# A decode block with attention and MLP: the last 64 columns of the output rows in shared products

## The chip, the cores and the metric

One NeuronCore of a Trainium2 chip runs the kernel. The metric is device time in microseconds (us), the median of several runs. The profile is one execution of the same program with the hardware profiler; its lines name an engine: PE is the matrix engine, PEld its weight loads, DVE the vector engine, ACT the scalar engine, POOL GpSimd, and SP the engine that only issues DMAs here. L483 is line 483 of the kernel before.

## What is computed

Two sequences (B = 2) with one new token each, D = 576. A gate g mixes an attention over a cache with an MLP:

```python
g = sigmoid((x * gate_w).sum(-1))
q = x @ wq                          # 32 heads of 128
p = softmax(q @ k_cache.T * 128**-0.5)   # 4096 cached keys a head
a = (p @ v_cache) @ wo              # 4096 -> 576
b = gelu(x @ w1 + b1) @ w2 + b2     # 576 -> 4608 -> 576
out = g * a + (1 - g) * b
```

Everything is float32. The two caches hold 134 MB each; with the weights 308.6 MB are read once.

## The kernel before

**The ring.** All large data pass through one SBUF tile, `ring`, of 49152 floats in each partition, in three slots of 16384 floats: 0 to 16383, 16384 to 32767, 32768 to 49151. First wq and w1 fill floats 0 to 39167. What lies behind them, from 39168 on, is handed out piece by piece by `temp()` (L159) to short-lived tiles of the first stage: x, the biases, transposes, the MLP's hidden row. They lie in the third slot.

**The order of the loads.** A list `seq` (L100 to L104) holds every load in order: wq, w1, then k and v of 16 units (a unit is four heads of one sequence, 8.4 MB of keys and as much of values), and three last loads with rows of w2 and wo. `load()` (L171) takes the next from the list and issues it on SP's queue. k of unit 0 (k0 below) goes to slot 0, v0 to slot 1, k1 to slot 2, v1 to slot 0 and so on. The first eight loads stand at fixed places in the program: five near the start, k0 at L298, v0 at L375 and k1 at L394. From then on `load_next` (L188) issues a load when the load three places before it, whose slot it takes, has been read for the last time.

**The order of the instructions** on each engine is the order of the program (a manual schedule). Accesses to parts of a tile that overlap are ordered by semaphores in the order of the program; parts that don't overlap are independent.

**The first stage** ends with the MLP's hidden values `hg` (L393), the load of k1 (L394), and a few small tiles (L396 to L407): `mod4`, `div4` and `hm` on DVE, a product of PE on the last two, and its copy `hx`. They split the last row group of w2 in four for the rows "wx". `mod4`, `div4` and `hm` have places of their own in pool `cp`. The gate sums L473 to L477 follow.

**The units** (L559 to L577): DVE multiplies the whole k slot by q in place (`mul`, L483), DVE and POOL sum over the head dimension (`red`, L487 to L489), a maximum goes over PE (L498) and DVE (L502), ACT exponentiates (L508), PE multiplies by v (`av`, L519, four groups of 32 output partitions in turn), and DVE and PE collect the result (L531, L537). In iteration i DVE does `mul` and `red` of unit i, PE `av` of unit i-1. v of unit i+1 takes the slot of k of unit i and is issued after `red(i)`; k of unit i+2 takes the slot of v of unit i and is issued after `av(i)`.

**The output rows.** w2 (36 rows of 576 columns in each partition, the last split as "wx") and wo (32 rows) come in the three last loads. Every row is multiplied by a weight of two columns, one for each sequence, and summed in PSUM tile `acc`. `acc_mm` (L351) splits the 576 columns in two products of 288; row r goes to partition groups 64 * (r % 2) and 32 behind it, so that four products in a row lie in four groups of 32 partitions. A float32 product is two instructions of PE in the profile. `mlp_out` and `wo_out` call it for w2 and wo; 24 of w2's rows stand ahead of `av` of the last unit, the others between the steps of the last normalization (L579 to L598).

**The end** (`last_out`, L435): `acc` is copied by ACT to `sums`; wo's rows from 23 on go to another tile `res` in four products of 144 columns each; after row 26 `fold` adds the four groups of `sums` to `res`; row 31 comes last, and copies and one DMA write the output. `late()` hands out places in the slot of the last load, behind its data.

Of the kernel before, what the change touches and what calls it, by code (L numbers as in the profile page):

```python
# [19 lines left out]
def kernel(  # L20
# [14 lines left out]
    nc = tc.nc  # L35
    B, H, SK, DH = k_cache.shape
    D = x.shape[-1]
# [21 lines left out]
    NC = 4  # L59
    DO = D // NC  # L60
    NS = 2
    DS = D // NS
    SCALE = float(DH) ** -0.5
    SLOTS = 3

    LAST = (
        (("w2", 0, 14), ("w2", 14, 28)),
        (("w2", 28, 35), ("wx", 0, 4), ("wo", 0, 9), ("wo", 9, 17)),
        (("wo", 17, 23), ("wo", 23, 27), ("wo", 27, 30), ("wo", 30, 31), ("wo", 31, 32)),
    )  # L70
    FOLD = 23
    SLOT = R * DH
# [8 lines left out]
    cp = ctx.enter_context(tc.tile_pool(name="cp", bufs=1))  # L81
# [4 lines left out]
    ps_acc = ctx.enter_context(tc.tile_pool(name="ps_acc", bufs=1, space=bass.MemoryType.PSUM))  # L86
    ps_av = ctx.enter_context(tc.tile_pool(name="ps_av", bufs=2, space=bass.MemoryType.PSUM))
    ps_big = ctx.enter_context(tc.tile_pool(name="ps_big", bufs=1, space=bass.MemoryType.PSUM))
    ps_o = ctx.enter_context(tc.tile_pool(name="ps_o", bufs=1, space=bass.MemoryType.PSUM))
# [6 lines left out]


    ring = rp.tile([P, SLOTS * SLOT], F32, name="ring")
    kt, vt, wqt, w1t, rows = {}, {}, {}, {}, {}
    seq = [(w, c) for w in ("wq", "w1") for c in range(len(ROWS[w]) + 1)]  # L100
    for i in range(N):
        seq += [("k", i), ("v", i)]
# [19 lines left out]
    def slot(n):  # L122
        k = len(held) % SLOTS
        return ring[:, k * SLOT:k * SLOT + n]
# [12 lines left out]
    def load_last(m):  # L137
        n = sum(z - a for _, a, z in LAST[m]) * D

        used["e"], used["z"] = len(held) % SLOTS * SLOT + n, (len(held) % SLOTS + 1) * SLOT  # L140
        t = slot(n)
        o = 0
        for w, a, z in LAST[m]:
            if w == "wx":
                x2 = t[:32, o:o + z * D]
                rows[w] = x2
                o += z * D
                for c in range(4):
                    nc.sync.dma_start(x2[c::4].rearrange("e (s n) -> e s n", s=4), srcx2[c])
                continue  # L150

            ends = (a * D, a * D + DS, a * D + DS + DO, z * D) if (w, z) == ("wo", 32) else (a * D, z * D)
            for u, v in zip(ends, ends[1:]):
                nc.sync.dma_start(t[:, o:o + v - u], srcs[w][:, u:v])
                o += v - u
            for r in range(a, z):
                rows[w, r] = t[:, o - (z - r) * D:o - (z - r - 1) * D]

    def temp(n, parts=P):  # L159
        t = ring[:parts, used["t"]:used["t"] + n]  # L160
        used["t"] += n
        assert used["t"] <= SLOTS * SLOT
        return t

    def late(n, parts=P):
        t = ring[:parts, used["e"]:used["e"] + n]
        used["e"] += n
        assert not seq and used["e"] <= used["z"]
# [28 lines left out]
    b2r = temp(D, 1)  # L197
# [17 lines left out]
    ident = cp.tile([P, P], F32, name="ident")  # L215
# [3 lines left out]
    idsc = cp.tile([P, P], F32, name="idsc")  # L219
    nc.vector.tensor_scalar_mul(idsc, ident, SCALE)  # L220

# [4 lines left out]
    NO = N * E  # L226
    pt = []
    for j in range(NPB):
        t = cp.tile([P, NT * EB + 32 - EB], F32, name=f"p{j}")
# [39 lines left out]
    g1 = cp.tile([P, B], F32, name="g1")  # L269
# [76 lines left out]

    acc = ps_acc.tile([P, DS], F32, name="acc")

    def acc_mm(lhsT, rhs, k, start=False, stop=False):  # L351
        m = lhsT.shape[-1]
        for s in range(NS):
            o = 64 * (k % 2) + 32 * s
            nc.tensor.matmul(  # L355
                acc[o:o + m], lhsT, rhs[:, s * DS:(s + 1) * DS], start=start, stop=stop, skip_group_check=True
            )

    g1z = cp.tile([1, 2, 32], F32, name="g1z")
    nc.vector.memset(g1z, 0.0)  # L360
    nc.vector.tensor_copy(g1z[:, 0, :B], g1[0:1])
    for k in range(2):
        acc_mm(g1z[:, k], b2r, k, start=True)

    fold = cp.tile([P, NS, B], F32, name="fold")
    nc.vector.tensor_add(
        fold, ident[:, :P // 2].rearrange("p (s c) -> p s c", s=NS)[:, :, :B],
        ident[:, P // 2:].rearrange("p (s c) -> p s c", s=NS)[:, :, :B],
    )


    hps = [ps_av.tile([P, 512], F32, tag="av", name=f"hps{m}") for m in range(FB - 1)]
# [12 lines left out]
    hg = cp.tile([P, NF, B], F32, name="hg")  # L385
    t = temp(NF * B).rearrange("p (r b) -> p r b", b=B)
# [6 lines left out]
    nc.vector.tensor_mul(hg, t, g1.unsqueeze(1).to_broadcast([P, NF, B]))  # L393
    load()  # L394

    mod4 = cp.tile([P, 4], F32, name="mod4")  # L396
    nc.vector.tensor_reduce(mod4, ident.rearrange("p (q s) -> p s q", s=4), AX.X, ALU.add)
    div4 = cp.tile([P, 32], F32, name="div4")
    nc.vector.tensor_reduce(div4, ident.rearrange("p (q s) -> p q s", s=4), AX.X, ALU.add)
    hm = cp.tile([P, 4, B], F32, name="hm")  # L400
    nc.vector.tensor_mul(
        hm, hg[:, NR:].to_broadcast([P, 4, B]), mod4.unsqueeze(2).to_broadcast([P, 4, B])
    )
# [2 lines left out]
    hx = cp.tile([32, 4, B], F32, name="hx")  # L406
    nc.vector.tensor_copy(hx.rearrange("p s b -> p (s b)"), hxps)  # L407

    def mlp_x():
        for s in range(4):  # L410
            acc_mm(hx[:, s], rows["wx"][:, s * D:(s + 1) * D], s)

    def mlp_out(lo, hi):
        for r in range(lo, hi):
            acc_mm(hg[:, r], rows["w2", r], r)

    KB = DH // 32
    oP = cp.tile([P, B, 32], F32, name="oP")  # L420

    def o_turn(turn):
        t = late(B * 32).rearrange("p (b c) -> p b c", c=32)
        for b in range(B):
            nc.vector.transpose(t[:, b], oT[:, b])
        ps = ps_sm.tile([P, B * 32], F32, tag="sm", name="op_t")
        nc.tensor.matmul(ps, turn, t.rearrange("p b c -> p (b c)"), start=True, stop=True)
        nc.vector.tensor_copy(oP.rearrange("p b c -> p (b c)"), ps)

    def wo_out(lo, hi):  # L430
        for r in range(lo, hi):
            acc_mm(oP[:, :, r], rows["wo", r], r)


    def last_out():  # L435
        res = ps_big.tile([32 * (NC - 1) + B, DO], F32, tag="big", name="res")
        sums = late(DS)
        nc.scalar.copy(sums, acc)

        def part(r, s):  # L440
            nc.tensor.matmul(  # L441
                res[32 * s:32 * s + B], oP[:, :, r], rows["wo", r][:, s * DO:(s + 1) * DO],
                start=r == FOLD, stop=r == 31, skip_group_check=True,
            )

        for r in range(FOLD, 31):
            for s in range(NC):
                part(r, s)
            if r == FOLD + 3:
                for s in range(NC):  # L450
                    h, o = divmod(s * DO, DS)
                    nc.tensor.matmul(
                        res[32 * s:32 * s + B], fold[:, h], sums[:, o:o + DO],
                        start=False, stop=False, skip_group_check=True,
                    )

        osb = late(D, B)
        for h in ((0, 1), (2,), (3,)):
            for s in h:
                part(31, s)  # L460
            for s in h:
                cpy = nc.vector.tensor_copy if s % 2 == 0 else nc.scalar.copy
                cpy(osb[:, s * DO:(s + 1) * DO], res[32 * s:32 * s + B])  # L463
        nc.sync.dma_start(out.rearrange("b s d -> (b s) d"), osb)
# [2 lines left out]
    st, mx, mt, bias, avs = {}, {}, {}, {}, {}  # L467
    oT = cp.tile([P, B, H], F32, name="oT")

    oall = ps_o.tile([NO, 512], F32, name="oall")  # L470
    gall = cp.tile([NO, 1], F32, name="gall")
    gsel = cp.tile([NO, B], F32, name="gsel")
    nc.vector.tensor_reduce(  # L473
# [85 lines left out]
    for i in range(N):  # L559
        k = i - 1  # L560
# [18 lines left out]
    k = N - 1  # L579
    max_n(k)  # L580
    softmax(k)
    mlp_out(0, 24)
    av(k)
    load_next(("v", k))
# [43 lines left out]
```

## Time and profile before

| what | us |
| --- | --- |
| median of 3 runs (722.96 to 723.07) | 723.01 |
| the profiled execution | 723.16 |
| its span, first to last instruction | 721.0 |
| DVE busy | 518.4 |
| PE busy | 237.9 |
| POOL busy | 143.2 |

The profiled execution takes 2.16 us more than its span. The busy times are unions over the span; the records of PE overlap each other, since products in different partition groups run beside one another. In lists of groups a line has the operation, its output and input tiles, its count, then busy time, mean ns of one, and the idle time of the engine just before it with what ended it. In a timeline a line has start, length, engine, line and operation; what stands in brackets is the idle time before it and its end.

### The profile page before, as it was taken

Reading aid. Unit: us, or ns where it says so; the run is one execution under the profiler, and the core shown is the slowest. Engines: PE = TensorE matmul, PEld = TensorE weight load, DVE = VectorE, ACT = ScalarE, POOL = GpSimd, SP = SyncE. Lnnn points to the kernel's source line nnn. Section 1 sums busy time; section 2 is a strip of 40 time slices with the busy share of each in tenths; the row PEclk is TensorE's granted clock in tenths of the full one; section 3 lists DMA queues with packets and bytes.
Section 4 is the critical chain, followed back from the end, with each engine's and each line's share of the span. In section 5 each row is a group of like instructions: output and inputs, shape, how many; then the busy total and the mean of one; then the engine's idle time right before and its main releaser. Section 6 shows DMA issues by size and latency. Waiting matters only on the chain.

```text
span 721.0 us, 3934 instructions
## 1 busy us (share of the span) xinstructions
PE 237.9 (33%) x1675; PEld 72.7 (10%) x1675; DVE 518.4 (72%) x154; ACT 37.8 (5%) x141; POOL 143.2 (20%) x28
## 2 busy tenths in 40 slices
PE   0754022240416060604142230506060603123197
PEld 0321000010101010101010000101010101000032
DVE  0004969889696969696969789696969596978810
ACT  0010010100001010101010100001010101010000
POOL 1000130404050404021130404040504012040400
PEclk9977557575757575655757575757575665757599
DMA  9999999999999999999999999999999999999996
GB/s 408 411 449 423 436 436 419 451 419 451 422 451 423 444 429 440 419 436 429 437 433 433 440 434 433 440 429 444 425 440 425 426 436 433 436 436 434 418 429 277
DMA packets 7261, 308.84 MB, mean 428 GB/s; under 512 B 830, under 2 KB 1214, under 8 KB 1612
## 3 DMA queue, kind: packets, MB, share of 16 engines
q1 hardware_dynamic: 7220, 308.55, 99.0%
q8 instruction: 13, 0.21, 0.1%
q10 hardware_dynamic: 24, 0.05, 0.0%
q14 instruction: 4, 0.03, 0.0%
HBM read 308.59 MB, written 0.00 MB: 428 GB/s over the span
## 4 chain that ended last, share of the span: by engine, by line
DMA 46%; DVE 35%; PE 17%; ACT 1%; issue 1%; POOL 0%; ACTq 0%; DVEq 0%; SPq 0%; POOLq 0%
DMA ring<-in_A_k_cache_dram 39%; DVE ring L483 19%; DVE s L488 10%; PE av L519 9%; DVE s L489 5%; DMA ring<-in_A_wo_dram 3%; DMA ring<-in_gate_w_dram 3%; PE hps L291 2%; PE qps L291 1%; PE oall L537 1%; PE acc L355 1%; PE mt L498 1%; DMA ring<-in_B_b_dram 1%; ACT p L508 1%; PE qps L316 0%
## 5 line engine op out<-in xcount | busy, mean ns | idle before, releaser
L483 DVE TENSOR_TENSOR ring<-ring,q 128x16384 f32<-128x16384 f32 x16 | 275.6, 17225 | 103.7 <-DMA ring<-in_A_k_cache_dram 103.7
L487 POOL TENSOR_TENSOR ring<-ring 128x3968 f32<-128x3968 f32 x16 | 137.0, 8564 | 488.7 <-DVE ring L483 488.7
L488 DVE TENSOR_REDUCE s<-ring 128x66 f32<-128x8448 f32 x16 | 143.3, 8953 | 1.3
L519 PE MATMUL av<-ring,p 128*32 128x512 f32 x1024 | 136.8, 694 | 11.4 <-ACT p L508 6.1
L498 PE MATMUL mt<-idsc,m 128*128 128x128 f32 x32 | 12.7, 500 | 359.8 <-DVE m L493 359.8
L489 DVE TENSOR_REDUCE s<-ring 128x62 f32<-128x3968 f32 x16 | 68.4, 4276 | 0.0
L508 ACT ACTIVATE p<-s,bs 32x128 f32<-32x128 f32 x64 | 25.5, 398 | 485.4 <-DVE bs L502 484.2
L519 PEld LDWEIGHTS av<-ring,p 128*32 128x32 f32 x1024 | 36.1, 126 | 121.8 <-issue 105.1
L498 PEld LDWEIGHTS mt<-idsc,m 128*128 128x128 f32 x32 | 8.0, 313 | 375.5 <-DVE m L493 314.2
L537 PE MATMUL oall<-avs,pick 128*64 128x512 f32 x32 | 30.6, 1059 | 0.8 <-DVE avs L531 0.8
L339 PE MATMUL qb<-qm,spread 64*128 64x512 f32 x8 | 7.3, 1014 | 70.4 <-POOL qm L335 70.4
L531 DVE TENSOR_TENSOR avs<-av,selr 128x512 f32<-128x512 f32 x16 | 10.9, 682 | 16.3 <-PE av L519 16.3
L249 DVE COPY ring<-ring 3x64 f32<-3x64 f32 x2 | 0.3, 182 | 19.1 <-DMA ring<-in_gate_w_dram 19.1
L378 DVE TENSOR_TENSOR ring<-hps,ring 128x384 f32<-128x384 f32 x3 | 1.7, 559 | 15.9 <-PE hps L291 15.7
L335 POOL TENSOR_TENSOR qm<-qall,mine 64x512 f32<-64x512 f32 x4 | 4.1, 1032 | 44.7 <-ACT qall L318 44.7
L310 DVE COPY ring<-ident 128x8 f32<-128x8 f32 x8 | 0.7, 169 | 15.5 <-DMA ring<-in_B_b_dram 15.5
L508 ACT ACTIVATION_READ_ACCUMULATOR p<-s,bs 32x1 f32 x64 | 11.8, 184 | 0.0
L291 PE MATMUL hps<-ring 128*32 128x384 f32 x120 | 11.5, 549 | 0.0
L355 PE MATMUL acc<-ring,hg 128*2 128x288 f32 x140 | 11.3, 467 | 0.0
L291 PE MATMUL qps<-ring 128*32 128x512 f32 x80 | 10.2, 668 | 0.0
L463 DVE COPY ring<-res 2x144 f32<-2x144 f32 x2 | 0.6, 300 | 13.1 <-PE res L441 13.0
L339 PEld LDWEIGHTS qb<-qm,spread 64*128 64x128 f32 x8 | 1.8, 279 | 73.4 <-POOL qm L335 73.4
(88 smaller groups left out, 76.3 us busy)
## 6 DMA issues: line engine op xcount, KB each, us to landing
ring<-in_B_w_dram SPq DMA_DIRECT2D x2, 4608.0 KB
ring<-in_B_w_dram SPq DMA_DIRECT2D x2, 4032.0 KB
ring<-in_A_wo_dram SPq DMA_DIRECT2D x1, 2592.0 KB
ring<-in_A_wo_dram SPq DMA_DIRECT2D x1, 2304.0 KB
ring<-in_B_w_dram SPq DMA_DIRECT2D x1, 2016.0 KB, 12.7
ring<-in_A_wo_dram SPq DMA_DIRECT2D x1, 1728.0 KB
ring<-in_B_w_dram SPq DMA_DIRECT2D x1, 1152.0 KB
ring<-in_A_wo_dram SPq DMA_DIRECT2D x1, 1152.0 KB, 19.0
```

The lines of the kernel that those rows point to most:

```text
L291: nc.tensor.matmul(ps[32 * j:32 * j + 32, :width], lhs, ts[c][:, o:o + width], start=(k == 0), stop=last, skip_group_check=True,)
L339: nc.tensor.matmul(ps, spread, t.rearrange("p u d -> p (u d)"), start=True, stop=True)
L355: nc.tensor.matmul(acc[o:o + m], lhsT, rhs[:, s * DS:(s + 1) * DS], start=start, stop=stop, skip_group_check=True)
L483: nc.vector.tensor_mul(kt[i], kt[i], qs[i].unsqueeze(1).to_broadcast([P, R, DH]))
L487: nc.gpsimd.tensor_add(t[:, :, :DH2], t[:, :, :DH2], t[:, :, DH2:])
L488: nc.vector.tensor_reduce(st[i][:, HALVED:], kt[i][:, HALVED:], AX.X, ALU.add)
L489: nc.vector.tensor_reduce(st[i][:, :HALVED], t[:, :, :DH2], AX.X, ALU.add)
L498: nc.tensor.matmul(mt[i], mx[i].to_broadcast([P, P]), idsc, start=True, stop=True)
L508: nc.scalar.activation(p[w, :, e * RB:(e + 1) * RB], st[i][w].rearrange("p (t c) -> p t c", c=RB), AF.Exp, bias=bias[i][w, e:e + 1], scale ...
L519: nc.tensor.matmul(ps[32 * j:32 * j + 32], p[:, EB * t:EB * t + 32], vt[i][:, RB * t:RB * (t + 1)].rearrange("p r d -> p (r d)"), start=(t ...
L531: nc.vector.tensor_mul(t, avs[i].rearrange("p (r d) -> p r d", d=DH), selr.unsqueeze(2).to_broadcast([P, RB, DH]))
L537: nc.tensor.matmul(oall, pick[:, NO - E - i * E:2 * NO - E - i * E], avs[i].rearrange("p r d -> p (r d)"), start=(i == 0), stop=(i == N - ...
```

## The change

**Products.** `acc` becomes 512 columns wide, and `acc_mm` issues one product of 512 columns for a row; row r goes to partition group 32 * (r % 4). The other 64 columns of up to eight rows go to `rest_mm`: one product with the weights of all these rows (2 columns a row, 16 for eight rows) and the 64 columns of each of them (512 for eight), into PSUM tile `part_r` at partition 0. Of its 16 by 512 results those with the same row on both sides are wanted. There are nine such products: five for w2, one for "wx", three for wo. In `last_out` DVE multiplies `part_r` by a mask `ownr` and sums over the rows, and one more small product (`foldr`) adds the result to the last 64 columns of `res`.

**Loads.** The boundary between the second last load and the last one moves from wo's row 17 to row 16, and that between the two DMAs for wo in the second last from row 9 to row 8.

**Places.** `g1z` comes from `temp()` ahead of the first loads of the caches. `mod4`, `div4` and `hm` come from `temp()` instead of `cp`; their lines stay where they are, behind the `load()` of k1. By the sizes of all pieces they take floats 46033 to 46076 of the ring. Some small tiles are new in `cp` (`b2t`, `foldr`, `ownr`), `fold` is smaller, and `res` shares a PSUM place with `oall`.

```diff
-        (("w2", 28, 35), ("wx", 0, 4), ("wo", 0, 9), ("wo", 9, 17)),
-        (("wo", 17, 23), ("wo", 23, 27), ("wo", 27, 30), ("wo", 30, 31), ("wo", 31, 32)),
+        (("w2", 28, 35), ("wx", 0, 4), ("wo", 0, 8), ("wo", 8, 16)),
+        (("wo", 16, 23), ("wo", 23, 27), ("wo", 27, 30), ("wo", 30, 31), ("wo", 31, 32)),
...
-    acc = ps_acc.tile([P, DS], F32, name="acc")
+    acc = ps_acc.tile([P, DM], F32, name="acc")
...
-        for s in range(NS):
-            o = 64 * (k % 2) + 32 * s
-            nc.tensor.matmul(
-                acc[o:o + m], lhsT, rhs[:, s * DS:(s + 1) * DS], start=start, stop=stop, skip_group_check=True
-            )
-
-    g1z = cp.tile([1, 2, 32], F32, name="g1z")
+        o = 32 * (k % 4)
+        nc.tensor.matmul(acc[o:o + m], lhsT, rhs[:, :DM], start=start, stop=False, skip_group_check=True)
+
+    g1z = temp(64, 1).rearrange("p (k c) -> p k c", k=2)
...
+    def rest_mm(lhsT, rhs, n):
+        start = not part_r
+        if start:
+            part_r.append(ps_big.tile([NB * B, DM], F32, tag="big", name="acc_r"))
+            assert n == NB
+        nc.tensor.matmul(
+            part_r[0][:n * B, :n * DR], lhsT, rhs[:, :, DM:], start=start, stop=False, skip_group_check=True
+        )
...
     load()
 
-    mod4 = cp.tile([P, 4], F32, name="mod4")
+    mod4 = temp(4)
     nc.vector.tensor_reduce(mod4, ident.rearrange("p (q s) -> p s q", s=4), AX.X, ALU.add)
-    div4 = cp.tile([P, 32], F32, name="div4")
+    div4 = temp(32)
     nc.vector.tensor_reduce(div4, ident.rearrange("p (q s) -> p q s", s=4), AX.X, ALU.add)
-    hm = cp.tile([P, 4, B], F32, name="hm")
+    hm = temp(4 * B).rearrange("p (s b) -> p s b", b=B)
...
             acc_mm(hg[:, r], rows["w2", r], r)
+            for a, z in ((0, 8), (8, 14), (14, 22), (22, 28), (28, 35)):
+                if r == z - 1:
+                    g = a - a % 14
+                    rest_mm(
+                        hg[:, a:z].rearrange("p r b -> p (r b)"), runs["w2", g][:, a - g:z - g], z - a
+                    )
...
-            acc_mm(oP[:, :, r], rows["wo", r], r)
+            acc_mm(oP[:, r], rows["wo", r], r)
+            for a, z in ((0, 8), (8, 16), (16, FOLD)):
+                if r == z - 1:
+                    rest_mm(oP[:, a:z].rearrange("p r b -> p (r b)"), runs["wo", a], z - a)
...
+        own = late(DM, NB * B).rearrange("p (r n) -> p r n", n=DR)
+        nc.vector.tensor_mul(
+            own, part_r[0].rearrange("p (r n) -> p r n", n=DR), ownr.unsqueeze(2).to_broadcast([NB * B, NB, DR])
+        )
+        tail = late(DR, NB * B)
+        nc.vector.tensor_reduce(tail, own.rearrange("p r n -> p n r"), AX.X, ALU.add)
```

More of the change, by code (lines that the diff above doesn't have):

```diff
@@ L62 @@
     DS = D // NS
+    DM = 512
+    DR = D - DM
+    NB = DM // DR
     SCALE = float(DH) ** -0.5
@@ L98 @@
     ring = rp.tile([P, SLOTS * SLOT], F32, name="ring")
-    kt, vt, wqt, w1t, rows = {}, {}, {}, {}, {}
+    kt, vt, wqt, w1t, rows, runs = {}, {}, {}, {}, {}, {}
     seq = [(w, c) for w in ("wq", "w1") for c in range(len(ROWS[w]) + 1)]
@@ L145, in load_last @@
                 x2 = t[:32, o:o + z * D]
-                rows[w] = x2
+                runs[w, 0] = x2.rearrange("p (r n) -> p r n", n=D)
                 o += z * D
@@ L155, in load_last @@
                 o += v - u
+            runs[w, a] = t[:, o - (z - a) * D:o].rearrange("p (r n) -> p r n", n=D)
             for r in range(a, z):
@@ L345, with acc_mm @@
     q_unit(0)
-    acc = ps_acc.tile([P, DS], F32, name="acc")
-    def acc_mm(lhsT, rhs, k, start=False, stop=False):
+    acc = ps_acc.tile([P, DM], F32, name="acc")
+    def acc_mm(lhsT, rhs, k, start=False):
         m = lhsT.shape[-1]
-        for s in range(NS):
-            o = 64 * (k % 2) + 32 * s
-            nc.tensor.matmul(
-                acc[o:o + m], lhsT, rhs[:, s * DS:(s + 1) * DS], start=start, stop=stop, skip_group_check=True
-            )
-    g1z = cp.tile([1, 2, 32], F32, name="g1z")
+        o = 32 * (k % 4)
+        nc.tensor.matmul(acc[o:o + m], lhsT, rhs[:, :DM], start=start, stop=False, skip_group_check=True)
+    g1z = temp(64, 1).rearrange("p (k c) -> p k c", k=2)
     nc.vector.memset(g1z, 0.0)
     nc.vector.tensor_copy(g1z[:, 0, :B], g1[0:1])
[L362 to L368, printed above, removed]
-    )
+    for k in range(4):
+        acc_mm(g1z[:, min(k, 1)], b2r, k, start=True)
+    b2t = cp.tile([1, DR], F32, name="b2t")
+    nc.vector.tensor_copy(b2t, b2r[:, DM:])
+    fold = cp.tile([P, B], F32, name="fold")
+    nc.vector.tensor_reduce(
+        fold, ident.rearrange("p (g c) -> p c g", g=4)[:, :B], AX.X, ALU.add
+    )
+    foldr = cp.tile([NB * B, B], F32, name="foldr")
+    nc.vector.tensor_reduce(
+        foldr, ident[:NB * B, :NB * B].rearrange("p (r b) -> p b r", b=B), AX.X, ALU.add
+    )
+    ownr = cp.tile([NB * B, NB], F32, name="ownr")
+    nc.vector.tensor_reduce(
+        ownr, ident[:NB * B, :NB * B].rearrange("p (r b) -> p r b", b=B), AX.X, ALU.add
+    )
+    part_r = []
+    def rest_mm(lhsT, rhs, n):
[6 more added lines that the diff above has]
+        )
+        if start:
+            nc.tensor.matmul(
+                part_r[0][:B, :DR], g1[0:1], b2t, start=False, stop=False, skip_group_check=True
+            )
     hps = [ps_av.tile([P, 512], F32, tag="av", name=f"hps{m}") for m in range(FB - 1)]
@@ L410, in mlp_x @@
         for s in range(4):
-            acc_mm(hx[:, s], rows["wx"][:, s * D:(s + 1) * D], s)
+            acc_mm(hx[:, s], runs["wx", 0][:, s], s)
+        rest_mm(hx.rearrange("p s b -> p (s b)"), runs["wx", 0], 4)
     def mlp_out(lo, hi):
@@ L415, in mlp_out @@
             acc_mm(hg[:, r], rows["w2", r], r)
+            for a, z in ((0, 8), (8, 14), (14, 22), (22, 28), (28, 35)):
[3 more added lines that the diff above has]
+                        hg[:, a:z].rearrange("p r b -> p (r b)"), runs["w2", g][:, a - g:z - g], z - a
+                    )
     KB = DH // 32
-    oP = cp.tile([P, B, 32], F32, name="oP")
+    oP = cp.tile([P, 32, B], F32, name="oP")
     def o_turn(turn):
@@ L427, in o_turn @@
         nc.tensor.matmul(ps, turn, t.rearrange("p b c -> p (b c)"), start=True, stop=True)
-        nc.vector.tensor_copy(oP.rearrange("p b c -> p (b c)"), ps)
+        nc.vector.tensor_copy(oP, ps.rearrange("p (b c) -> p c b", b=B))
     def wo_out(lo, hi):
         for r in range(lo, hi):
-            acc_mm(oP[:, :, r], rows["wo", r], r)
+            acc_mm(oP[:, r], rows["wo", r], r)
+            for a, z in ((0, 8), (8, 16), (16, FOLD)):
+                if r == z - 1:
+                    rest_mm(oP[:, a:z].rearrange("p r b -> p (r b)"), runs["wo", a], z - a)
     def last_out():
-        res = ps_big.tile([32 * (NC - 1) + B, DO], F32, tag="big", name="res")
-        sums = late(DS)
+        res = ps_o.tile([32 * (NC - 1) + B, DO], F32, tag="o", name="res")
+        sums = late(DM)
         nc.scalar.copy(sums, acc)
+        own = late(DM, NB * B).rearrange("p (r n) -> p r n", n=DR)
+        nc.vector.tensor_mul(
+            own, part_r[0].rearrange("p (r n) -> p r n", n=DR), ownr.unsqueeze(2).to_broadcast([NB * B, NB, DR])
+        )
+        tail = late(DR, NB * B)
+        nc.vector.tensor_reduce(tail, own.rearrange("p r n -> p n r"), AX.X, ALU.add)
         def part(r, s):
             nc.tensor.matmul(
-                res[32 * s:32 * s + B], oP[:, :, r], rows["wo", r][:, s * DO:(s + 1) * DO],
+                res[32 * s:32 * s + B], oP[:, r], rows["wo", r][:, s * DO:(s + 1) * DO],
                 start=r == FOLD, stop=r == 31, skip_group_check=True,
@@ L450, in last_out @@
                 for s in range(NC):
-                    h, o = divmod(s * DO, DS)
+                    n = min(DO, DM - s * DO)
                     nc.tensor.matmul(
-                        res[32 * s:32 * s + B], fold[:, h], sums[:, o:o + DO],
+                        res[32 * s:32 * s + B, :n], fold, sums[:, s * DO:s * DO + n],
                         start=False, stop=False, skip_group_check=True,
                     )
+                nc.tensor.matmul(
+                    res[32 * s:32 * s + B, n:], foldr, tail, start=False, stop=False, skip_group_check=True,
+                )
         osb = late(D, B)
@@ L468 @@
     oT = cp.tile([P, B, H], F32, name="oT")
-    oall = ps_o.tile([NO, 512], F32, name="oall")
+    oall = ps_o.tile([NO, 512], F32, tag="o", name="oall")
     gall = cp.tile([NO, 1], F32, name="gall")
```

## The prediction, as it was put on record

> **What bounds the kernel now.** I read the page first: its table of queues, the chain that ended last, then the waits and the stages.
>
> ```profile
> span 721.0 us, 3934 instructions
> q1 hardware_dynamic: 7220, 308.55, 99.0%
> DMA 46%; DVE 35%; PE 17%; ACT 1%; issue 1%; POOL 0%; ACTq 0%; DVEq 0%; SPq 0%; POOLq 0%
> DVE ring L483 <- DMA ring<-in_A_k_cache_dram: 103.7, 16, 8.3
> ```
>
> SP's queue keeps the DMA engines busy for 99.0% of the span, and the big multiplication of DVE (L483) waits for keys ahead of each of the 16 units, 103.7 us together. The span is the time of the transfers. The DVE and PE pieces in the chain are the releases of slots, not a bound of their own. The stages show whether there is a hole in the transfers anywhere in the first units (columns: window and length, busy of PE, PEld, DVE, ACT, POOL, granted PE clock, DMA share, GB/s):
>
> ```profile
> 90.00:109.00 19.00, 5.33 (x30) 1.70 (x34) 11.33 (x4) 1.96 (x8) 6.26 (x1) 0.52 1.01 438
> 109.00:128.00 19.00, 4.38 (x44) 1.00 (x36) 18.92 (x2) 0.00 (x0) 1.59 (x1) 0.75 1.02 442
> 147.00:186.00 39.00, 11.45 (x80) 3.27 (x76) 31.55 (x6) 1.96 (x8) 8.56 (x1) 0.65 1.01 436
> ```
>
> There is none. A time in which the DMA engines have nothing to do is therefore lost: no later stage has room to make it up. A faster PE gains nothing in the units. So two places matter: what holds back a load, and the last microseconds after the last rows have landed.
>
> **The first stage: three small tiles behind the load of k1.** The change moves `mod4`, `div4` and `hm` into the ring at floats 46033 to 46076. The third slot is 32768 to 49151, and k1 is loaded into all of it; the load (L394) stands ahead of the three in the program. The timeline where it happens, and SP's wait for that load:
>
> ```profile
> 66.27 0.23 DVE L393 TENSOR_TENSOR hg<-ring,g 128x72 f32<-128x72 f32 x1
> 66.42 0.37 DVE L397 TENSOR_REDUCE mod<-ident 128x4 f32<-128x128 f32 x1
> 66.71 0.33 SPq L130 DMA_DIRECT2D ring<-in_A_k_cache_dram  x1
> 66.90 0.15 DVE L401 TENSOR_TENSOR hm<-hg,mod 128x8 f32<-128x8 f32 x1
> 67.93 0.15 DVE L477 TENSOR_REDUCE gall<-gsel 64x1 f32<-64x2 f32 x1
> 70.34 17.23 DVE L483 TENSOR_TENSOR ring<-ring,q 128x16384 f32<-128x16384 f32 x1 [2.27 <-DMA ring<-in_A_k_cache_dram]
> 100.78 0.33 SPq L130 DMA_DIRECT2D ring<-in_A_v_cache_dram  x1
> 109.05 17.23 DVE L483 TENSOR_TENSOR ring<-ring,q 128x16384 f32<-128x16384 f32 x1 [6.74 <-DMA ring<-in_A_k_cache_dram]
> 113.45 0.33 SPq L130 DMA_DIRECT2D ring<-in_A_k_cache_dram  x1
> 147.61 17.22 DVE L483 TENSOR_TENSOR ring<-ring,q 128x16384 f32<-128x16384 f32 x1 [6.59 <-DMA ring<-in_A_k_cache_dram]
> SPq L130 <- DVE hg L393: 7.0, 1, 7.0
> ```
>
> SP's wait shows that overlaps inside the ring are tracked: the load of k1 waited 7.0 us for the last read of the old pieces of that slot. Today `mod4` runs at 66.42 us, while that load is still to be issued. In the ring it is a write to a place that a load ahead of it in the program fills, so it must wait until k1 has landed: at 109.05 us, where today `mul(1)` starts on exactly that event. (k1 then holds 44 foreign floats of 16384 in each partition; that changes no duration.)
>
> The added wait stands in DVE's queue. Behind it, in order, are `div4`, `hm`, `hx`, the gate sums and `mul(0)`, though k0 has been there since 70.34. The stretch from `mod4` to the end of `gall` takes 66.42 to 68.08 = 1.66 us, so `mul(0)` starts at 109.05 + 1.66 = 110.7 instead of 70.34. From `mul(0)` to the issue of v1, which needs slot 0, are 100.78 - 70.34 = 30.44 us; v1 is issued at 141.15. v0 and k1 were the last transfers in the queue, so from k1's landing at 109.05 SP has nothing to issue: a hole of 32.1 us. To it comes the start of a transfer on idle engines, for which the nearest row is the small output store at the end:
>
> ```profile
> 718.66 0.29 SPq L464 DMA_DIRECT2D out_dram<-ring  x1
> ```
>
> From its issue to the end of the span are 721.0 - 718.66 = 2.34 us. As a start and a completion outside the stream I take 2.0 us, with 0 and 2.4 as the ends. The loss is 32.1 + 2.0 = 34.1 us.
>
> Does the next stage give some back? k2 needs slot 1 and so `av(0)`: issued 113.45 - 100.78 = 12.67 us after v1, at 153.8. Two transfers take 147.61 - 109.05 = 38.56 us, one 19.3; v1 lands at 162.5, so k2 waits in the queue without a hole and lands at 181.7. `mul(1)` follows `red(0)` at once, near 142.5, and frees k1's slot 30.4 us later, at 173, ahead of 181.7: v2 is in time too. `mul(2)` starts at 181.7 instead of 147.61, +34.1, and from there on the pattern is that of before. Nothing is given back.
>
> **The last stage.** Times here are those of before; the shift comes on top.
>
> ```profile
> 684.72 7.86 PE L355 MATMUL acc<-ring,hg 128*2 128x288 f32 x96
> 692.41 7.04 PE L519 MATMUL av<-ring,p 128*32 128x512 f32 x64
> 700.27 1.07 PE L537 MATMUL oall<-avs,pick 128*64 128x512 f32 x2 [0.82 <-DVE avs L531]
> 706.21 4.53 PE L355 MATMUL acc<-ring,oP 128*2 128x288 f32 x68
> 711.55 1.64 PE L355 MATMUL acc<-ring,oP 128*2 128x288 f32 x24 [0.80 <-DMA ring<-in_A_wo_dram]
> 714.29 1.17 PE L441 MATMUL res<-ring,oP 128*2 128x144 f32 x32 [1.10 <-DMA ring<-in_A_wo_dram]
> 715.27 0.43 PE L452 MATMUL res<-ring,fold 128*2 128x144 f32 x8
> 716.37 1.95 PE L441 MATMUL res<-ring,oP 128*2 128x144 f32 x40 [0.67 <-DMA ring<-in_A_wo_dram]
> ```
>
> A product is two records, and four products in the four partition groups run side by side. I count in turns of four: 64 records of 512 columns are 8 turns in 7.04, 0.88 us a turn; 68 records of 288 are 8.5 turns in 4.53, 0.53 a turn. A single product of 512 columns (two records) takes 1.07 us, as long as a whole turn. So a row costs a quarter of 0.88 = 0.22 us after the change against half of 0.53 = 0.27 before: 0.05 us less. But a shared product (`rest_mm`) always goes to the first group, and the next row there, and in the queue all behind it, waits for it: it takes a turn of its own, 0.88 us for eight rows, 0.11 a row. The change makes PE slower by some 0.06 us a row.
>
> Counted by what the first group has to do one after the other: ahead of `av(15)` 6 rows and 3 shared products, 9 turns x 0.88 = 7.9 us against 12 x 0.53 = 6.4: +1.5, a little more at the lower clock with which the stretch begins:
>
> ```profile
> 684.00:688.00 4.00, 4.00 (x29) 0.99 (x32) 0.00 (x0) 1.30 (x6) 0.00 (x0) 0.50 0.96 413
> 692.00:694.00 2.00, 2.00 (x28) 0.62 (x24) 0.00 (x0) 0.00 (x0) 0.00 (x0) 1.00 1.06 439
> ```
>
> I take +1.8. From there to the last row that is multiplied ahead of the wait at 711.55: rows 24, 28 and 32 of w2, two shared products, "wx" one and a half, wo four rows and two shared, 12.5 turns = 11.0 us, against 64 products of 288, 16 turns = 8.5 us: +2.5. PE, which ended at 706.21 + 4.53 = 710.74, comes to wo's row 16 at 715.0; its rows landed at 711.55. Rows 16 to 22 with their shared product are 3 turns, 2.6 us, to 717.7, against 713.19 before. Now rows 23 to 26 (1.17 us) to 718.8. Beside them lie the copy of `acc` and DVE's mask and sum, which the kernel before doesn't have. Nearest rows:
>
> ```profile
> 699.52 0.69 DVE L531 TENSOR_TENSOR avs<-av,selr 128x512 f32<-128x512 f32 x1 [16.30 <-PE av L519]
> 701.71 0.68 DVE L549 TENSOR_REDUCE ring<-oall 64x128 f32<-64x512 f32 x1
> 713.25 0.40 ACT L438 COPY ring<-acc 128x288 f32<-128x288 f32 x1 [27.90 <-PE acc L355]
> ```
>
> Both of DVE's have 512 elements a partition: 0.69 + 0.68 (ends: 0.3 for both, 1.6), plus hand-overs, to 719.2. `fold` and `foldr` 0.43, to 719.6; rows 27 to 30 as 23 to 26, 1.17, to 720.8; the first half of row 31 0.15, to 720.9. Today that point is 716.37 + 1.95 = 718.3. So the end, which the rows' landing sets today, is set by PE: +2.6 us. If PE's extra stays under the slack it is 0; if each shared product costs the lone 1.07 us, the eight up to there give 8 x 0.19 = 1.5 more, with slower DVE steps 4.5.
>
> The moved loads cost nothing: the last load's issue waits for `av(15)`, now 1.8 us later, but the queue holds work:
>
> ```profile
> 696.07 20.26 DMA ring<-in_A_wo_dram
> ```
>
> This piece of the chain was issued at 696.07 and landed 20.26 us later, behind others. The row that goes to the last load is under 1 us of transfer. If that cover were gone, 1.8 us would come on top. The new small products and reductions around 45 us lie on engines that wait (PE's next weights land later), v0 waits in a queue, and `mod4`'s wait takes up any delay there.
>
> **Sum.** 34.1 + 2.6 = 36.7 us on the profiled run's 723.16, 2.16 above its span: 759.9. The median is 0.15 lower: **759.7**.
>
> **The rule that speaks against the last stage.** The Trainium skill, "TensorEngine Tiling (Array Packing)", section "Instruction Overhead", says that each matmul carries an overhead of about 60 cycles, so that fewer and wider products gain. The change issues some 50 products fewer up to the last row of `acc`, and at that price (an estimate from the page, with the 2.4 GHz that the Trainium skill, "TensorE: Matmul & The Clock Gate", gives ahead of its Part 1, and two records each) saves 2.5 us of PE. The last stage would then cost nothing, as in rival 1. Here the two turns, 0.53 and 0.88, leave 0.08 a turn when drawn down to no columns, 0.02 us a product, and that is in my turns already.
>
> **Rivals.**
> 1. *The wait alone, the last stage hidden.* A shared product runs beside its neighbours (its group is otherwise free) or products cost by count (at 0.53 / 4 = 0.13 us each, 50 fewer are 6.6 us less), so PE still comes before the landed rows. For it: up to `acc`'s last row 124 products become 72. Against: 1.07 us for a lone product. 723.0 + 34.1 = 757.1.
> 2. *Last stage dearer:* shared products alone on PE and a slow mask and sum; 34.1 + 4.5 and more: 761.7 to 765. Against it, DVE's rows have the same sizes.
> 3. *No wait.* `mod4` isn't held until k1 lands, because what matters is that k1's issue follows the old readers; DVE runs at 66.42 as today. SP's 7.0 us speaks against it: the tracking sees parts of the ring. Then only the last stage is left, 725.6.
> 4. *No wait, and nothing at the end, not slower:* as 3, while shared products fill gaps of the first group and PE keeps its 0.80 us of idle time before 711.55. It decides if a turn with a shared product costs under 0.3 us. The end is the landing of the last rows: 723.0. It can't be faster, since these landings set the end already.
>
> **Chances.** Forecast 0.72, rival 1 0.14, rival 2 0.06, rival 3 0.05, rival 4 0.03. The range: low end the hole with no start (32.1) and a hidden last stage, 755.1; high end 34.5 and 4.5 on 723.0, 762.0, with a little for DVE's unknown steps: 755 to 763. A measurement of this kernel can tell about 0.2% from no change. Slower by more 0.96, the same 0.03, faster 0.01.
>
> **What would show it.** In the profile after: `mod4`'s reduction with some 42 us of idle time before it, released by the DMA of the key cache; the first L483 multiplication near 110.7, the third near 181.7; a DMA share far below 0.9 between 109 and 141; v1 issued near 141. At the end: the copy of `acc` some 4 us later against the landing of the rows, and no wait of PE for the last rows. Wrong I would be if the first multiplication still starts at 70, or if `mul(2)` is later by clearly less than 32 us, which means that a part of the lost time comes back.

## The result and the profile after

| kernel | median us | runs | ratio to the kernel before, 95% interval |
| --- | --- | --- | --- |
| before | 722.99 (721.78 to 723.32) | 6 | 1 |
| changed | 759.87 (759.52 to 760.31) | 6 | 1.0515 (1.0501 to 1.0528) |

The forecast was 759.7. The six runs of the kernel before lie in two groups, 721.8 to 721.9 and 723.0 to 723.3. The profiled execution of the changed kernel took 760.03 with a span of 757.9. From the page of the changed kernel, the same lines as of the one before, with the strip of DMA shares in 40 slices and the group of the moved tile:

```profile
span 757.9 us, 3736 instructions
DMA  9999960599999999999999999999999999999996
q1 hardware_dynamic: 7220, 308.55, 94.3%
L423 DVE TENSOR_REDUCE ring<-ident 128x4 f32<-128x128 f32 x1 | 0.4, 377 | 39.5 <-DMA ring<-in_A_k_cache_dram 39.5
```

The bytes are those of before, but the queue fills 94.3% of the span and not 99.0%. The strip shows where: one slice of 18.9 us is empty, its two neighbours are about half full, and everything else is at 9 but for the very last slice, which was at 6 before as well. And one instruction of 0.4 us, the reduction for `mod4`, has 39.5 us of idle time ahead of it, ended by the DMA of the keys. Around the hole, from the timeline of the changed kernel:

```profile
69.48 0.33 SPq L133 DMA_DIRECT2D ring<-in_A_k_cache_dram  x1
108.77 0.38 DVE L423 TENSOR_REDUCE ring<-ident 128x4 f32<-128x128 f32 x1 [39.49 <-DMA ring<-in_A_k_cache_dram]
110.28 0.15 DVE L522 TENSOR_REDUCE gall<-gsel 64x1 f32<-64x2 f32 x1
110.36 17.21 DVE L528 TENSOR_TENSOR ring<-ring,q 128x16384 f32<-128x16384 f32 x1
140.77 0.33 SPq L133 DMA_DIRECT2D ring<-in_A_v_cache_dram  x1
142.22 17.21 DVE L528 TENSOR_TENSOR ring<-ring,q 128x16384 f32<-128x16384 f32 x1
153.54 0.33 SPq L133 DMA_DIRECT2D ring<-in_A_k_cache_dram  x1
183.33 17.23 DVE L528 TENSOR_TENSOR ring<-ring,q 128x16384 f32<-128x16384 f32 x1 [9.15 <-DMA ring<-in_A_k_cache_dram]
```

k1 is issued at 69.48, `mod4` waits for its landing, `mul(0)` follows at 110.36 and v1 is issued at 140.77 (forecast: 110.7 and 141.15). `mul(1)` then finds its keys in place; `mul(2)` waits, as in every unit before the change, and is 183.33 - 147.61 = 35.7 us late (forecast: 34.1). The same stretch as stages (window and length, busy times by engine, PE clock, DMA share, GB/s):

```profile
104.00:105.00 1.00, 0.00 (x0) 0.00 (x0) 0.00 (x0) 0.00 (x0) 0.00 (x0) 0.50 1.96 852
105.80:106.00 0.20, 0.00 (x0) 0.00 (x0) 0.00 (x0) 0.00 (x0) 0.00 (x0) 0.50 1.51 655
106.00:141.60 35.60, 0.67 (x4) 0.60 (x4) 31.79 (x11) 0.00 (x0) 8.56 (x1) 0.50 0.00 0
141.60:142.00 0.40, 0.38 (x2) 0.08 (x1) 0.00 (x0) 0.00 (x0) 0.00 (x0) 0.50 4.45 1475
```

A window counts a packet whole if the packet starts in it, which is why shares over 1 occur. So the last packets of k1 start before 106.0, and none starts for 35.6 us, until 141.6. The row from 105.8 to 106.0 holds 0.20 us x 655 GB/s = 131 KB in 1.51 x 16 x 0.20 = 4.8 us of engine time; as two packets of 65.5 KB, a partition's part of k1 each, that is 2.4 us for one, so by this estimate bytes still move up to some 108.4. At the end, again from the timeline of the changed kernel (with the start of `av(15)`, the product with the values of the last unit):

```profile
727.52 0.63 PE L564 MATMUL av<-ring,p 128*32 128x512 f32 x3
745.33 0.59 PE L389 MATMUL acc_r<-ring,oP 128*16 128x512 f32 x1
745.34 0.60 PE L358 MATMUL acc<-ring,oP 128*2 128x512 f32 x3
745.76 0.59 PE L389 MATMUL acc_r<-ring,oP 128*16 128x512 f32 x1
745.77 2.30 PE L358 MATMUL acc<-ring,oP 128*2 128x512 f32 x13
747.91 0.59 PE L389 MATMUL acc_r<-ring,oP 128*16 128x512 f32 x1
750.72 0.59 ACT L474 COPY ring<-acc 128x512 f32<-128x512 f32 x1 [30.77 <-PE acc L358]
751.44 0.68 DVE L476 TENSOR_TENSOR ring<-acc_r,ownr 16x512 f32<-16x512 f32 x1 [9.82 <-PE acc_r L389]
752.15 1.01 DVE L480 TENSOR_REDUCE ring<-ring 16x64 f32<-16x512 f32 x1
753.22 0.27 PE L498 MATMUL res<-ring,foldr 16*2 16x64 f32 x2 [0.59 <-DVE ring L480]
753.41 1.41 PE L483 MATMUL res<-ring,oP 128*2 128x144 f32 x40
755.53 0.29 SPq L509 DMA_DIRECT2D out_dram<-ring  x1
```

No matrix product here waits for a DMA any more; the brackets behind L441 and L355 that named wo's loads are gone. PE waits once, 0.59 us, for DVE's sum. The output is issued at 755.53, 36.87 us later than before. The turns can be read off as well: from one shared product (745.33) to the next (747.91) are 2.58 us, three turns of 0.86, with 16 records of rows, which are eight rows or two turns, between them. The third turn is the shared product's.

### The profile page after: what moved, and what is told of

Same layout as the page of the kernel before. It is cut to its first block, busy times and chain, and to the rows that moved or that the text cites. A ratio compares the mean times of both kernels' runs of the same rounds, so it can differ in the third digit from the quotient of the medians.

```text
span 757.9 us, 3736 instructions
## 1 busy us (share of the span) xinstructions
PE 241.2 (32%) x1573; PEld 71.1 (9%) x1573; DVE 520.3 (69%) x159; ACT 38.1 (5%) x141; POOL 143.2 (19%) x28
## 3 DMA queue, kind: packets, MB, share of 16 engines
q1 hardware_dynamic: 7220, 308.55, 94.3%
## 4 chain that ended last, share of the span: by engine, by line
DMA 41%; DVE 38%; PE 19%; issue 1%; ACT 1%; POOL 0%; ACTq 0%; DVEq 0%; SPq 0%; POOLq 0%
DMA ring<-in_A_k_cache_dram 37%; DVE ring L528 20%; DVE s L533 11%; PE av L564 9%; DVE s L534 5%; DMA ring<-in_gate_w_dram 3%; PE acc L358 2%; PE qps L295 2%; PE hps L295 2%; PE oall L582 1%; PE mt L543 1%; DMA ring<-in_B_b_dram 1%; ACT p L553 1%; PE acc_r L389 1%; PE qps L320 0%
## 5 line engine op out<-in xcount | busy, mean ns | idle before, releaser
L564 PEld LDWEIGHTS av<-ring,p 128*32 128x32 f32 x1024 | 36.1, 125 | 119.9 <-issue 103.5
L423 DVE TENSOR_REDUCE ring<-ident 128x4 f32<-128x128 f32 x1 | 0.4, 377 | 39.5 <-DMA ring<-in_A_k_cache_dram 39.5
L358 PE MATMUL acc<-ring,hg 128*2 128x512 f32 x70 | 12.0, 669 | 0.0
```

The lines of the kernel that those rows point to most:

```text
L358: nc.tensor.matmul(acc[o:o + m], lhsT, rhs[:, :DM], start=start, stop=False, skip_group_check=True)
L564: nc.tensor.matmul(ps[32 * j:32 * j + 32], p[:, EB * t:EB * t + 32], vt[i][:, RB * t:RB * (t + 1)].rearrange("p r d -> p (r d)"), start=(t ...
```

## Experiments

Two questions are open although the time came out: whether the wait does its harm through what is queued behind it, and whether the sum is right in its terms. The main theory ("queue") says that the 0.4 us tile costs a hole because `mul(0)` and with it v1 stand behind it in DVE's queue. Its rivals: the wide and shared products, or writing into a slot, cost time themselves. For the end, the "turn" theory says that shared products stop PE's queue; the "mask" theory that DVE's mask and sum make the end late.

### The load behind the tiles

```diff
     nc.vector.tensor_mul(hg, t, g1.unsqueeze(1).to_broadcast([P, NF, B]))
-    load()
...
     nc.vector.tensor_copy(hx.rearrange("p s b -> p (s b)"), hxps)
+    load()
```

> The changed kernel with the load of k1 moved behind hx, so that the three small tiles are written before it is issued; products and end stay as changed. Queue theory (the hole in the transfers comes from mul(0) and v1 standing behind the waiting tile): the 34.6 us of the units go, the last stage's +2.3 stays: 725.3 (724.5 to 726.2). k1 is issued about 1 us later than in the kernel before, covered by v0 in the queue. Rival, the wide and shared products or the new layout slow the stream or PE in the units too: clearly over 727.

Measured: 725.26 us, ratio 1.0034 (1.0022 to 1.0047). The places in the ring stay, `load()` moves down behind the copy `hx`, and the hole is gone: 34.6 of the 36.9 us. In this kernel's timeline the load of k1 waits for the tiles, and not the other way round:

```profile
70.18 0.37 DVE L421 TENSOR_REDUCE ring<-ident 128x4 f32<-128x128 f32 x1
71.24 0.33 SPq L133 DMA_DIRECT2D ring<-in_A_k_cache_dram  x1
71.71 17.21 DVE L527 TENSOR_TENSOR ring<-ring,q 128x16384 f32<-128x16384 f32 x1
```

What is left, 725.26 - 722.99 = 2.3 us, is the cost of the products and of what else comes with them, without the hole (forecast: 2.6).

### The places alone

```diff
-    mod4 = cp.tile([P, 4], F32, name="mod4")
+    mod4 = temp(4)
...
-    div4 = cp.tile([P, 32], F32, name="div4")
+    div4 = temp(32)
...
-    hm = cp.tile([P, 4, B], F32, name="hm")
+    hm = temp(4 * B).rearrange("p (s b) -> p s b", b=B)
```

> The kernel before with mod4, div4 and hm alone taken from the ring behind the load of k1 (44 floats of k1 in each partition are overwritten); products and end as before. Queue theory: the hole alone, 34.6 of it: 757.5 (756.5 to 758.5). Rival, the hole needs the changed products: 723 to 725.

Measured: 759.13, ratio 1.0503 (1.0489 to 1.0517): three lines in the kernel before, no product touched, and nearly the whole loss. The rival that needs the products falls. But 759.13 lies above the range that I had given, 756.5 to 758.5: 36.1 us is more than the 34.6 that I had taken from the changed kernel's last unit, so the parts don't add up: 36.1 + 2.3 = 38.4 against 36.9. I come back to this.

### The same wait, later in the queue

```diff
+    def split_hx():
+        mod4 = temp(4)
...
             softmax(k)
+        if i == 1:
+            split_hx()
         st[i] = sp.tile([P, R], F32, tag="s", name=f"s{i}")
```

> The changed kernel with mod4, div4, hm and hx moved in the program to iteration 1, between the softmax of unit 0 and mul(1); the same places, so they still wait for the landing of k1. Queue theory (the price is what stands behind the waiting tile): v1 is issued near 103 as before, the tile waits some 6 us beside the wait that mul(1) has anyway, mul(1) starts 1.7 us later, no hole: 725.3 (724.5 to 726.5). Rival, a wait of DVE for a landing or a write into a slot under load costs by itself: 731 or more.

Measured: 725.20, ratio 1.0035 (1.0022 to 1.0047). The tiles are written into the slot that k1 has just filled, and DVE waits for it:

```profile
100.71 0.33 SPq L133 DMA_DIRECT2D ring<-in_A_v_cache_dram  x1
108.89 0.38 DVE L426 TENSOR_REDUCE ring<-ident 128x4 f32<-128x128 f32 x1 [6.71 <-DMA ring<-in_A_k_cache_dram]
110.03 17.23 DVE L530 TENSOR_TENSOR ring<-ring,q 128x16384 f32<-128x16384 f32 x1
118.81 0.33 SPq L133 DMA_DIRECT2D ring<-in_A_k_cache_dram  x1
```

The wait is there, 6.71 us for the same landing at 108.9. But v1 was issued at 100.71, ahead of it, and k2 only has to be issued before v1's bytes run out. It costs nothing that the kernel with the load behind doesn't cost too. (`mul(1)` would have waited for this landing in any case.) The wait has no price of its own; the price is that of the load that stands behind it in DVE's queue.

### Another slot: a shorter hole

```diff
-    mod4 = temp(4)
+    in_v0 = ring[:, SLOT + 13265:SLOT + 13309]
+    mod4 = in_v0[:, :4]
```

(`div4` and `hm` take the floats behind it.)

> The changed kernel with the three tiles in the second slot, which v0 fills (44 floats of v0 are overwritten), in place of the third. They wait for the landing of v0, about 89.6, not of k1. Queue theory: mul(0) starts near 91.3, v1 is issued near 121.7, k1 has landed at 109: a hole of 12.7 us and the same start of the stream as in the changed kernel, 2 to 2.6: 15 of shift and 2.3 at the end, 740.3 (738.5 to 741.5). Rival, the price is fixed (a disturbed order of slots): 759.9.

Measured: 740.53, ratio 1.0251 (1.0236 to 1.0267). The price follows the landing that is waited for; it isn't fixed.

```profile
89.90 0.38 DVE L424 TENSOR_REDUCE ring<-ident 128x4 f32<-128x128 f32 x1 [20.33 <-DMA ring<-in_A_v_cache_dram]
121.90 0.33 SPq L133 DMA_DIRECT2D ring<-in_A_v_cache_dram  x1
164.56 17.23 DVE L529 TENSOR_TENSOR ring<-ring,q 128x16384 f32<-128x16384 f32 x1 [8.96 <-DMA ring<-in_A_k_cache_dram]
```

With it the start of the stream on idle engines can be measured twice. From v1's issue to `mul(2)` are 164.56 - 121.90 = 42.7 us here and 183.33 - 140.77 = 42.6 in the changed kernel, against 38.56 for two transfers in the running stream: a stop and a start cost 4.0 to 4.1 us, with a hole of some 13 us between k1's landing (taken at 109, as in the other profiles) and v1's issue as with one of 32. The prediction took 2.0.

### The shared products in turn

A counter of products takes the place of the row number; a shared product waits until the counter comes to group 0 and takes that place. Based on the kernel with the load behind.

```diff
+    def turn_next():
+        if late_rest and count[0] % 4 == 0:
+            rest_now(*late_rest.pop(0))
+            count[0] += 1
+        count[0] += 1
+        return count[0] - 1
...
+        if not start:
+            k = turn_next()
         o = 32 * (k % 4)
```

> As the kernel with the load behind hx, and the shared products wait until the rotation of the four partition groups comes to group 0 and take that place; the rows take the next group. Turn theory (a shared product stops the queue for a whole turn because the next row wants the same group): up to the last row 18 turns of 0.88 in place of 24.5, PE is 5 us earlier and reaches wo's row 16 before it has landed; the end is the landing again: 723.0 (722.5 to 723.6). Mask theory (the end is late because of the copy, DVE's mask and sum and the last small product after the rows): nearly all of +2.3 stays, 724.8 to 725.3.

Measured: 723.65, ratio 1.0011 (1.0002 to 1.0020). 1.6 of the 2.3 us are gone without a product less, so the turns are the larger part. The expectation's 723.0 was missed by 0.65, its upper end by 0.05. The timeline shows that a shared product no longer has a turn to itself, and two things that I had not counted:

```profile
692.47 0.59 PE L578 MATMUL av<-ring,p 128*32 128x512 f32 x1
707.68 0.92 PE L402 MATMUL acc_r<-ring,hg 128*14 128x448 f32 x2
711.23 0.59 PE L402 MATMUL acc_r<-ring,oP 128*16 128x512 f32 x1
712.95 0.59 PE L402 MATMUL acc_r<-ring,oP 128*16 128x512 f32 x1
715.75 0.68 DVE L490 TENSOR_TENSOR ring<-acc_r,ownr 16x512 f32<-16x512 f32 x1 [9.63 <-PE acc L371]
716.46 1.01 DVE L494 TENSOR_REDUCE ring<-ring 16x64 f32<-16x512 f32 x1
717.53 0.27 PE L512 MATMUL res<-ring,foldr 16*2 16x64 f32 x2 [0.64 <-DVE ring L494]
719.84 0.29 SPq L523 DMA_DIRECT2D out_dram<-ring  x1
```

From 711.23 to 712.95 are 1.72 us, two turns for one shared product and seven rows, against the three turns for one and eight rows in the changed kernel. But w2's last shared product falls between two rows of "wx" and stands alone for 0.9 us, so PE comes to the last rows later than the 18 turns promise. And PE still waits 0.64 us for DVE's mask and sum, 1.7 us together.

### The end without mask and sum

```diff
-        nc.vector.tensor_mul(
-            own, part_r[0].rearrange("p (r n) -> p r n", n=DR), ownr.unsqueeze(2).to_broadcast([NB * B, NB, DR])
-        )
+        nc.vector.tensor_copy(own[:, 0, :1], part_r[0][:, DM - 1:])
...
-        nc.vector.tensor_reduce(tail, own.rearrange("p r n -> p n r"), AX.X, ALU.add)
+        nc.vector.memset(tail, 0.0)
```

> As the kernel with the load behind hx, without DVE's mask and sum over the shared products (the last 64 columns then lack the rows below 23 and the bias). Turn theory: PE waits 0.6 us less for the last small product, 724.7 (724.3 to 725.0). Mask theory: all of it goes, 723.0.

Measured: 724.96, ratio 1.0032 (1.0020 to 1.0044), 0.3 below the kernel with the load behind and far from 723.0. The direction is that of the turn theory, but 0.3 is inside the spread of both kernels (724.0 to 725.7). The mask theory falls as the whole cause: with the mask and the sum gone and the turns kept, most of the loss stays. The traces tell more than these times. The start of `av(15)` and the issue of the output, in the kernel with the load behind:

```profile
691.93 0.73 PE L563 MATMUL av<-ring,p 128*32 128x512 f32 x3
719.94 0.29 SPq L508 DMA_DIRECT2D out_dram<-ring  x1
```

and without mask and sum:

```profile
693.14 0.63 PE L561 MATMUL av<-ring,p 128*32 128x512 f32 x3
720.49 0.29 SPq L506 DMA_DIRECT2D out_dram<-ring  x1
```

These are 28.01 and 27.35 us, so mask and sum do cost 0.66 behind `av(15)`; in turn it is 719.84 - 692.47 = 27.37, so there the turns cost as much. The turns cost more ahead of `av(15)`: from w2's first row to `av(15)` are 8.68 us without mask and sum and 7.76 in turn, at nearly the same mean granted clock of PE (0.80 and 0.78). That clock is also what blurs the times: with the load behind, the same stretch in the same order takes 7.31 us at a mean clock of 0.95.

### In turn, and the sums added after row 30

```diff
-            if r == FOLD + 3:
+            if r == FOLD + 7:
```

> As the kernel with the shared products in turn, and the sums of the four groups and of the mask are added after row 30, not after row 26. There the 0.6 us that PE waits for DVE's sum lies beside the landing of the last rows. If the 0.66 us left in the kernel in turn is this wait, all is back: 723.0 (722.6 to 723.4). If it is PE that comes too late to row 16, it stays at 723.6.

Measured: 723.14 against 722.85 for the kernel before on that chip, ratio 1.0007 (0.9999 to 1.0016): no difference that can be told. PE waits for the landing again:

```profile
716.22 1.17 PE L497 MATMUL res<-ring,oP 128*2 128x144 f32 x32 [0.80 <-DMA ring<-in_A_wo_dram]
```

The interval overlaps that of the kernel in turn, so the gain over it is shown by the trace (no wait for DVE's sum is left) and not by the times. So the products of the change can be had at no cost that can be told, and they bring nothing: the last rows' landing sets the end, as in the kernel before. No version here beats that kernel, and the chain of waits says why: the span is the time of the transfers, and the change moves no byte less.

### The end beside the hole

Three kernels on one chip, to see why 36.1 and 2.3 don't add up: the changed one again, the places alone again, and the changed one with its hole but with the products in turn.

> The changed kernel again, on the chip of the next one: 759.9.

> The kernel before with the three places alone, again. If the end costs 2.2 us beside the hole too, it is 2.2 below the changed kernel, 757.7; if it costs 0.7, 759.1.

> The changed kernel, wait and hole included, with the shared products in turn. If the end costs its 2.2 us beside the hole as without it, 757.7 to 758.4 (1.6 less than the changed kernel). If the landing of the last rows is the later of the two beside the hole, as the 0.7 us between the changed kernel and the places alone hint, no more than 0.7 goes: 759.1 to 759.6.

Measured: 759.85 (ratio 1.0514, 1.0500 to 1.0529), 758.55 (1.0496, 1.0481 to 1.0510) and 758.59 (1.0497, 1.0483 to 1.0512). The changed kernel is above the places alone by 1.3 us (0.7 in the first pair), not by 2.3, and the products in turn take away 1.3. The last two times lie between the values that I had set for the two cases, so neither case came out as stated. The trace of the second run of the places alone shows where the rest is hidden (wo's rows 17 to 22):

```profile
747.48 1.64 PE L355 MATMUL acc<-ring,oP 128*2 128x288 f32 x24 [1.96 <-DMA ring<-in_A_wo_dram]
```

With the hole, PE waits 1.96 us for these rows (1.97 in the first run), against 0.80 in the kernel before. The rows land about 1.2 us later against PE's work than without the hole, and that much of PE's lateness costs nothing. From the start of the program the rows come 747.48 - 711.55 = 35.9 us later, which is the hole with its stop and start, 32.0 + 4.0. It is PE's work that is less late: in both runs of the places alone the last multiplication is only 35.1 us later, because a step of the stream that the kernel before has ahead of it is missing (last section).

## Why the prediction was right

**The bound.** Right. Lost transfer time isn't made up: `mul(2)` is 35.7 us late and, thirteen units on, the last multiplication starts at 685.84 against 651.25, 34.6 late.

```profile
570.11 17.23 DVE L528 TENSOR_TENSOR ring<-ring,q 128x16384 f32<-128x16384 f32 x1 [6.92 <-DMA ring<-in_A_k_cache_dram]
685.84 17.23 DVE L528 TENSOR_TENSOR ring<-ring,q 128x16384 f32<-128x16384 f32 x1 [6.64 <-DMA ring<-in_A_k_cache_dram]
```

```profile
651.25 17.23 DVE L483 TENSOR_TENSOR ring<-ring,q 128x16384 f32<-128x16384 f32 x1 [6.62 <-DMA ring<-in_A_k_cache_dram]
```

Up to `mul(12)`, at 570.11 against 534.03, it is still 36.1 late. The 1.6 us go at the next multiplication, all at once, where the kernel before has the step of the last section.

**The wait.** Right in mechanism and place: shown by the places alone (nearly the whole loss from three lines), by the load behind (the loss gone with the places kept) and by the later wait (the wait kept, the loss gone). The issue of v1 was forecast to 0.4 us, and the hole between landing and issue, 32.1, is 140.77 - 108.77 = 32.0.

**The start of a transfer.** Mis-sized: 2.0 us in the sum, with 2.4 as the upper end; 4.0 and 4.1 measured. The row that I had taken, a store of 4.5 KB, wasn't near enough to a load of 8.4 MB. The stages show where the time goes. The last packets of k1 start before 106.0, and the landing is seen at 108.77, 2.8 us later; v1 is issued at 140.77, and its first packets start after 141.6, 0.8 us or more later. In the running stream the packets of the next load start in such times; here none was in the queue. So no packet starts for 35.6 us, and `mul(2)` is 35.7 us late.

**The end.** The mechanism was right, a turn for each shared product, with DVE's mask and sum behind the last one. Alone it costs 2.3 us against 2.6 forecast, but inside it two sizes were off, in opposite directions. Ahead of `av(15)` I counted 6.4 us for the kernel before, although the row that I show for these products has 7.86. Counted from the start of the last multiplication, `av(15)` starts 41.2 us on before and 41.7 after (41.1 when the changed kernel ran again): at most some 0.5 later, and not 1.8. So the copy of `acc` comes 750.72 - 685.84 = 64.9 us after that start (64.3 in the second run) against 62.0 before: 2.3 to 2.9 later, and not 4.5. From the copy to the output I had 3.6 us (717.7 to 718.66 + 2.6), and it took 755.53 - 750.72 = 4.8: the mask starts 0.7 after the copy, since the last shared product ends after the last row, and the sum takes 1.01 and not 0.68. That 2.6 came so near 2.3 is in part luck. Beside the hole the end costs 0.7 to 1.3, since the rows land later there. I had set both terms side by side and added them.

**The sum.** So 34.1 + 2.6 = 36.7 stands against some 35.9 (36.1 and 35.7) + 1.0: 36.9. The hole was too small by about 1.8 and the end too large by about 1.6. That the total hit to 0.2 us is luck: the two errors cancel; either alone (761.5 or 758.1) would have stayed within the range, but not as near.

**The rule.** The Trainium skill, "TensorEngine Tiling (Array Packing)", section "Instruction Overhead", gives each matmul an overhead of about 60 cycles, and by my estimate from it the fewer products would have made the end free. These runs don't bear that out: the kernel with the load behind has fewer products and is 2.3 us slower. The product count didn't decide, the place in the rotation did, and mask and sum. With the places in turn the same count costs 0.66 us, and with the sums added later nothing that can be told.

## What to carry to other kernels

Scratch memory that lies in a buffer under load is free only up to the line that issues the load. Behind that line even a 0.4 us write waits for the whole transfer, and its price is the hole it makes for whatever its engine would have released, here 32 us of transfers and 4 more for the stop and the start; so when a small tile changes its place, compare its line with the loads of that place, or move the load down. And when products rotate over partition groups, a product more must take a place in the rotation, or it stops the queue for a whole turn, here 0.86 us.

## What the runs showed of the hardware that was not expected

Stopping and restarting the stream of 8.4 MB loads cost 4.0 us after 32 us of idle time and 4.1 after some 13. And the stream has a step: in the kernel before the distance of two multiplications is 38.6 us as a rule and 40.16 once, which no hole explains and which the changed kernel doesn't have at that place.

```profile
534.03 17.23 DVE L483 TENSOR_TENSOR ring<-ring,q 128x16384 f32<-128x16384 f32 x1 [6.72 <-DMA ring<-in_A_k_cache_dram]
574.19 17.23 DVE L483 TENSOR_TENSOR ring<-ring,q 128x16384 f32<-128x16384 f32 x1 [8.26 <-DMA ring<-in_A_k_cache_dram]
```

It isn't an accident of one execution. All six profiled kernels without a hole have it between the same two multiplications, `mul(12)` and `mul(13)`, with 39.9 to 40.2 us. In the six with a hole (five of 32 us, one of 13) this distance is 38.5. So the hole reads as 36 us up to `mul(12)`, as some 35 at the last multiplication, and as 36 again where the last rows land. What makes the step, and why the last rows are back at 36, stays open. Terms below 1.5 us can't be added up from single profiles of such a kernel, unless both ends of the stretch lie where no landing and no change of the clock comes between.
